# The branch rests in the last step of a half block, in the middle stage of a spectral/long-convolution kernel

## The chip, the cores and the metric

The kernel runs on one core of a Trainium2 chip. The core has a matrix engine (TensorE, PE in the profile; its weight loads are listed apart as PEld), a vector engine (VectorE, DVE), a scalar engine (ScalarE, ACT), a general engine (GpSimd, POOL) and an engine that here only issues transfers (SyncE, SP). Each engine works through its own instructions in order; semaphores tie the engines together. The metric is the time of the whole program on the device in microseconds, as the median of several runs.

## The reference

Four layers are applied to `x` of 2048 rows by 576 columns, twice the same pair. Layer A adds the real part of a two-dimensional Fourier transform of the normalised rows, done with given cosine and sine matrices. Layer B takes the normalised rows as a gate on a long causal convolution that doesn't depend on `x` at all:

```python
def _A_ref(x, dft_seq_re, dft_seq_im, dft_hid_re, dft_hid_im):
    a = jnp.einsum("bsd,ed->bse", x, dft_hid_re)
    b = jnp.einsum("bsd,ed->bse", x, dft_hid_im)
    return jnp.einsum("ts,bse->bte", dft_seq_re, a) - jnp.einsum("ts,bse->bte", dft_seq_im, b)

def _B_ref(q, k, v, shift_k, ssm_k, ssm_D):
    ...                     # k_shift: causal convolution of k, 4 taps
    kv = k_shift * v
    ...                     # y: causal convolution of kv with ssm_k, 2048 taps, by FFT
    y = y + kv * ssm_D[None, None, :]
    return q * y

x = x + _A_ref(_layernorm(x, axis=-1), ...)
x = x + _B_ref(_layernorm(x, axis=-1), ...)
x = x + _A_ref(_layernorm(x, axis=-1), ...)
x = x + _B_ref(_layernorm(x, axis=-1), ...)
```

## The kernel before

**Layer A in steps.** `layer` computes the sequence transform first. The 2048 output rows are four blocks of 512 (`tb`); each block has a half with the cosine matrix and a half with the sine matrix (`g`); each half block has 16 steps (`k`), numbered through as `n`, so that `n % 16` is the place in the half block and `n % 32 == 15` is the last step of a cosine half. A step multiplies one 128-row strip of `x` with one 128x512 piece of the matrix. Every operand is split in a rounded high part and a low part, so a step is 14 matmuls of 512 columns: three into each of the four accumulators (`s` in the profile) and two into a fifth (`rm`) for the 64 columns that are left over. There is one set of these accumulators. After the last step of a half, `evac_u` and `evac_r` move them to `u`, a high and a low part each: ScalarE copies (line 99), VectorE subtracts (line 100).

**The matrix pieces.** `load_c` asks for the piece of two steps ahead, through SP's queue (line 169 in the profile, `flts<-in_c_mat`, 256 KB), into one of two raw buffers; `split` then writes the high part on ScalarE (`mats<-flts`, line 99) and the low part on VectorE (`mats<-flts`, line 100) into one of three split buffers (`cs`). A raw buffer is free when VectorE's subtraction has read it; a split buffer is free when PE has finished the step that used it.

**The hidden transform.** When both halves of a block are there, `hidden` multiplies `u` with the second matrix: eight pieces of 27 matmuls a block (`bk<-w,u`), which `finish` lays between the steps of the next block.

**The branch.** `branch` is a generator that computes layer B's convolution beside layer A, since it needs no `x`. Its middle stage, which runs beside steps 47 to 111, has 64 "mid" feeds and 32 "i2" feeds. A mid feed is nine matmuls of 288 columns (`bk<-mid`, three each in `mid_kernel`, `mid_signal` and `mid_inverse`); ScalarE copies the results out of the accumulators (line 514, `flts<-bk`), moves half rows across (`flts<-flts`, 64x288, two of them) and splits (`mid<-flts`, 128x288 and 128x576); VectorE does lines 532 to 535 and the low parts of both splits (line 520). Feeds are read from DRAM through SP's queue (`flts<-td`, `mid<-td`), some feeds ahead, into a ring of land buffers; a land buffer is free when line 520 has read it. The copy `flts<-bk` of `mid_kernel` writes one of two `kk` buffers.

**What sets the order.** The generator of the layer yields inside each step: after the first and third accumulator ("part"), after the second (False) and at the end (True); in a last step after the second accumulator and at the end only. At each yield the program adds a share of the step to `passed`: 3/14, 3/14, 3/14 and 5/14 of `STEP` = 3.2, and 6/14 and 8/14 in a last step, times the weight in `BORDER` for that place. A finished hidden piece adds 3.6. Then the branch is advanced while its own count `spent` is under `work` times `passed / total`. The framework's scheduler makes each engine's final order from this, and may put neighbouring instructions in another order than the text has them; what it puts out is fixed when the program is built.

In the last step of a cosine half, `layer` also yields None while hidden pieces are left, and each such piece advances the branch too; that holds for any weight of `BORDER`.

Of the kernel before, what the change touches and what calls it, by code (L numbers as in the profile page):

```python
# [19 lines left out]
J = S // P  # L20
# [20 lines left out]
I2_END = 111  # L41
PREP = 113
MID_LAG = 1
BORDER = {J - 1: 0.5, 0: 0.75}
I2_FIRST = 37
I2_LATE = 6
I2_COST = 2.0
# [1 line left out]
STEP = 3.2  # L49
# [17 lines left out]
def fnet_h3_kernel(ctx: ExitStack, tc: tile.TileContext, x, c_mat, w_re, w_im, k_pad, v, shift_k,  # L67
# [34 lines left out]
    @contextmanager  # L102
    def behind(*instructions):
        with ExitStack() as stack:
            for i in instructions:
                stack.enter_context(tc.issue_after(i))
            yield
# [11 lines left out]
    def region_b(dt, name):  # L119
        return sb.tile([P, 6 * WIDE], dt, tag="rb", name=name)  # L120
# [11 lines left out]
    def lay(t, at, *sizes):  # L132

        for name, words, n in sizes:
            ring.setdefault(name, Ring()).tiles.extend(t[:, at + i * words:at + (i + 1) * words] for i in range(n))
            at += n * words
        assert at <= t.shape[1], (at, t.shape, sizes)
        return at

    def fresh(*names):  # L140
        for name in names:
            ring[name] = Ring()
# [150 lines left out]
    def finish(pending, pieces):  # L293
        while pending and pieces:
            if not isinstance(pending[0], types.GeneratorType):
                pending[0] = hidden(*pending[0])
            if next(pending[0], 0) == 0:
                pending.pop(0)
            else:
                pieces -= 1  # L300
# [432 lines left out]
    def advance(j=None):  # L733
        while to_store:
            load_after(*to_store.pop(0))
        with behind(*halved, *added, *evac):
            for row in list(making):
                if next(row, 0) == 0:
                    making.remove(row)
            if j is not None:  # L740
                making.append(make_x1(j))
                next(making[-1])
# [48 lines left out]
    for n, whole in layer(get_x0, lambda j: x[:, j, :], done0, pending):  # L791
        part = whole == "part"
        if part:
            whole = False
        if (whole or whole is not None and n % J < J - 1) and n <= F1_END and not part:
            at = n if whole else n - 0.5
            at16 = 4 + 2 * F1_16
            want = int(4 + F1_16 * at / 8 if at <= 16 else at16 + (68 - at16) * (at - 16) / (F1_END - 16))
            with behind(made[min(n + 2, J - 1)], *evac):
                while used < want:  # L800
                    next(br)
                    used += 1
        if whole is not None and not part and n >= W_FROM and len(W) < 9:
            with behind(*stored):
                next(wl)
        if whole and n == MID_LOAD:
            with behind(*asked):
                next(br)
        if n >= MID_FROM:
            if whole is not None:  # L810
                share = (5 if whole else 3) if n % J < J - 1 else (8 if whole else 6)
                passed += STEP * share / 14 * BORDER.get(n % J, 1.05)
            if whole is None or whole and n % 2 == 1 and n % (2 * J) < J - 1 and pending:
                finish(pending, 1)
                passed += PIECE
            while spent < work * min(1.0, passed / total):
                with behind(*added, *evac):
                    spent += next(br, work)
        if not whole:
            continue  # L820
        if n >= W_SAVE and n % 2 == 0:
            next(wl, 0)
        m = n - PREP
        if m == 0:
            lay(flts, SC_AT + CRAW * NT + 2 * D, ("xa", D, 2), ("yb", D, 2))
            old = ring["craw"]
            held = [old(), old()]
            fresh("craw")
            lay(flts, SC_AT + CRAW * NT + 6 * D, ("craw", NT, 1))
            ring["craw"].tiles.extend(held)  # L830
            gate = region_b(F32, "gate")
            lay(gate, 0, ("xa", D, 4), ("yb", D, 4), ("xj", D, 2))
        if 0 <= m and n < HOLD:
            advance(m // 2 if m % 2 == 0 and m < 2 * EARLY else None)
# [340 lines left out]
```

## Time and profile before

| | us |
|---|---|
| median of 3 runs | 1184.4 (1183.72 to 1184.5) |
| profiled execution, time | 1184.35 |
| profiled execution, span from first to last instruction | 1182.6 |
| middle stage in that span (steps 48 to 110) | about 250 to 604 |
| PE busy | 1168.9 (99% of the span) |
| VectorE busy | 866.5 (73%) |
| ScalarE busy | 647.7 (55%) |

Times in views of the trace are counted from the start of the span. A row of the chain or of a timeline gives its start, its length, the engine, the line and the tiles written and read, then the count; in brackets stands the idle time of the engine before it and what ended it. PE's matmuls overlap, so their listed lengths (about 0.39 us for 512 columns) are longer than the distance from one to the next; distances are read from the starts. `PEclk` is the share of full clock that PE was granted.

### The profile page before, as it was taken

The numbers are of one execution on the slowest core, as the hardware profiler recorded it, in microseconds if no ns is written. First come the engines' busy times: TensorE is split into PE (matmuls) and PEld (weight loads), VectorE is DVE, ScalarE is ACT, GpSimd is POOL, SyncE is SP. The second block draws the span as 40 slices with busy tenths as digits, with TensorE's granted clock in tenths as the row PEclk, the third lists the DMA queues.
The fourth block names the chain that finished last, engine by engine and source line by source line (L and its number), as shares of the span: only waits on it lengthen the run. The fifth ranks groups of instructions, "written<-read, shape, count | busy, mean of one in ns | idle before, by whom it ended". The sixth has DMA issues, their size and how long they took to land.

```text
span 1182.6 us, 18124 instructions
## 1 busy us (share of the span) xinstructions
PE 1168.9 (99%) x6198; PEld 990.9 (84%) x6198; DVE 866.5 (73%) x1564; ACT 647.7 (55%) x1280; POOL 75.5 (6%) x115
## 2 busy tenths in 40 slices
PE   8999999999999999999999999999999999999997
PEld 6776667987888988888888898888888888889997
DVE  7899984687777778877756765865776777774674
ACT  8855655577766667766645666534444445450210
POOL 2310000000000000001101111000000000001111
PEclk9999999999999999999999999999999999999999
DMA  9879898455766766648956777762772777895631
GB/s 331 290 235 310 270 300 283 146 158 156 216 201 192 211 181 189 187 142 237 287 188 213 250 242 236 250 242 79 253 247 72 236 269 257 264 322 158 198 108 40
DMA packets 147453, 255.64 MB, mean 216 GB/s; under 512 B 16161, under 2 KB 56353, under 8 KB 147362
## 3 DMA queue, kind: packets, MB, share of 16 engines
q1 hardware_dynamic: 111890, 210.17, 56.1%
q10 hardware_dynamic: 28560, 37.91, 9.1%
q0 software_dynamic: 6912, 6.43, 2.4%
q8 instruction: 48, 0.79, 0.3%
q14 instruction: 43, 0.35, 0.1%
HBM read 187.80 MB, written 66.65 MB: 215 GB/s over the span
## 4 chain that ended last, share of the span: by engine, by line
PE 92%; DMA 3%; DVE 2%; ACT 2%; issue 1%; SPq 0%; POOL 0%; DVEq 0%; ACTq 0%
PE s L76 54%; PE bk L76 30%; PE rm L76 6%; PE bf L76 3%; DMA flts<-in_c_mat 1%; DMA flts<-in_ssm_k 1%; DMA t<-ud 1%; ACT flts L514 1%; DMA early<-in_x 0%; DVE u L100 0%; DVE mats L100 0%; DVE mid L520 0%; ACT flts L453 0%; DMA flts<-td 0%; ACT mid L514 0%
## 5 line engine op out<-in xcount | busy, mean ns | idle before, releaser
L76 PE MATMUL s<-mats 128*128 128x512 f32 x2102 | 549.8, 395 | 3.1 <-ACT mats L197 1.6
L76 PEld LDWEIGHTS s<-mats 128*128 128x128 f32 x2102 | 383.1, 189 | 83.7 <-issue 10.8
L100 DVE TENSOR_TENSOR mats<-flts,mats 128x512 fp32r<-128x512 f32 x206 | 140.9, 688 | 58.7 <-ACT mats L99 57.3
L99 ACT ACTIVATE mats<-flts 128x512 fp32r<-128x512 f32 x206 | 128.4, 628 | 87.8 <-PE bk L76 30.2
L76 PE MATMUL bk<-mid 128*128 128x288 f32 x704 | 132.6, 303 | 2.6 <-ACT flts L514 2.2
L76 PEld LDWEIGHTS bk<-mid 128*128 128x128 f32 x704 | 111.5, 189 | 24.3 <-ACT flts L514 6.3
L514 ACT ACTIVATE flts<-bk 128x288 f32<-128x288 f32 (+1 forms) x192 | 78.3, 408 | 95.9 <-PE bk L76 80.4
L76 PE MATMUL bk<-w,u 128*128 128x288 f32 x864 | 119.9, 295 | 0.1
L76 PEld LDWEIGHTS bk<-w,u 128*128 128x128 f32 x864 | 117.5, 188 | 2.9 <-ACT flts L514 0.6
L520 DVE TENSOR_TENSOR mid<-flts,mid 128x576 fp32r<-128x576 f32 (+1 forms) x149 | 92.5, 624 | 9.1 <-ACT mid L514 6.7
L76 PE MATMUL rm<-mats 128*128 128x512 f32 x304 | 94.5, 391 | 0.0
L514 ACT ACTIVATE mid<-flts 128x576 fp32r<-128x576 f32 (+1 forms) x148 | 79.6, 574 | 3.5 <-DMA flts<-vd 1.6
L289 DVE TENSOR_TENSOR flts<-flts,bk 128x288 f32<-128x288 f32 x48 | 21.7, 453 | 69.1 <-PE bk L76 69.1
L76 PE MATMUL bk<-mats 128*128 128x288 f32 (+1 forms) x376 | 67.8, 317 | 0.0
L76 PEld LDWEIGHTS rm<-mats 128*128 128x128 f32 x304 | 57.0, 188 | 12.2 <-issue 0.2
L453 ACT ACTIVATE flts<-bf 128x384 f32<-128x384 f32 (+1 forms) x104 | 43.2, 461 | 43.9 <-PE bf L76 41.0
L76 PE MATMUL s<-t,mats 128*128 128x512 f32 x264 | 65.3, 390 | 0.3 <-DVE t L100 0.3
L186 POOL TENSOR_TENSOR flts<-flts 128x1 f32<-128x1 f32 x34 | 28.0, 823 | 517.6 <-DVE flts L185 515.2
L76 PE MATMUL bk<-mats,t 128*128 128x288 f32 (+1 forms) x368 | 59.3, 303 | 0.0
L76 PEld LDWEIGHTS s<-t,mats 128*128 128x128 f32 x264 | 49.4, 188 | 11.3 <-DVE t L100 0.8
L514 ACT ACTIVATE flts<-flts 64x288 f32<-64x288 f32 x128 | 56.6, 442 | 3.9
L76 PEld LDWEIGHTS bk<-mats 128*128 128x128 f32 x376 | 55.5, 188 | 3.4
(152 smaller groups left out, 1495.5 us busy)
## 6 DMA issues: line engine op xcount, KB each, us to landing
flts<-in_c_mat SPq DMA_DIRECT2D x148, 256.0 KB, 3.5
ph<-in_c_mat SPq DMA_DIRECT2D x54, 512.0 KB, 4.4
flts<-in_c_mat SPq DMA_DIRECT2D x30, 512.0 KB, 5.2
flts<-td SPq DMA_DIRECT2D x53, 288.0 KB, 3.1
td<-flts ACTq DMA_DIRECT2D x36, 384.0 KB, 4.3
vd<-flts ACTq DMA_DIRECT2D x64, 144.0 KB, 2.6
flts<-vd SPq DMA_DIRECT2D x32, 288.0 KB, 4.4
ud<-ph ACTq DMA_DIRECT2D x12, 512.0 KB, 6.4
```

What stands on the lines that cost most here:

```text
L76: return nc.tensor.matmul(ps, lhsT, rhs, start=first, stop=last, skip_group_check=more).ins
L99: a = nc.scalar.activation(h, src, AF.Copy).ins
L100: return a, nc.vector.tensor_tensor(l, src, h.bitcast(F32), OP.subtract).ins
L186: pows.append(nc.gpsimd.tensor_tensor(rs, ve, mhalf, OP.pow).ins)
L289: added[:] = [nc.vector.tensor_tensor(r[:, cs], r[:, cs], ps[:, :HD], OP.add).ins]
L453: stored[:] = [nc.scalar.activation(so[:, i, :], ps[i], AF.Copy).ins]
L514: last_act.append(nc.scalar.activation(*args, **kw).ins)
L520: nc.vector.tensor_tensor(l, src, h.bitcast(F32), OP.subtract)
```

## The change

Two weights of the shares change. The branch's weight in the last step of a half block goes from 0.5 to 0, the weight in the first stays at 0.75, and in the 14 others it goes from 1.05 to 1.085. A half block sums to 0.5 + 0.75 + 14 x 1.05 = 15.95 before and 0 + 0.75 + 14 x 1.085 = 15.94 now. Step 47, where the middle stage begins, is itself a last step.

```diff
-BORDER = {J - 1: 0.5, 0: 0.75}
+BORDER = {J - 1: 0.0, 0: 0.75}
...
                 share = (5 if whole else 3) if n % J < J - 1 else (8 if whole else 6)
-                passed += STEP * share / 14 * BORDER.get(n % J, 1.05)
+                passed += STEP * share / 14 * BORDER.get(n % J, 1.085)
```

No instruction is added or removed. What moves is the order.

The first place at which the orders part is just behind step 47. There, VectorE has the last subtraction of the fifth accumulator (`u<-flts`, 64x512), the four lines 532 to 535 of a branch feed, the two kinds of line 520, and the low parts of the matrix pieces (`mats<-flts`). Before:

```order
L100 TENSOR_TENSOR u<-flts,u 64x512
L532 SCALAR_TENSOR_TENSOR flts<-bk,flts 64x288
L520 TENSOR_TENSOR mid<-flts,mid 128x288
L533 TENSOR_TENSOR flts<-bk,flts 64x288
L534 TENSOR_TENSOR flts<-bk,flts 128x288
L520 TENSOR_TENSOR mid<-flts,mid 128x576
L535 TENSOR_TENSOR flts<-flts 128x288
L100 TENSOR_TENSOR mats<-flts,mats 128x512
L532 SCALAR_TENSOR_TENSOR flts<-bk,flts 64x288
L100 TENSOR_TENSOR mats<-flts,mats 128x512
```

VectorE at the same place now:

```order
L100 TENSOR_TENSOR u<-flts,u 64x512
L532 SCALAR_TENSOR_TENSOR flts<-bk,flts 64x288
L100 TENSOR_TENSOR mats<-flts,mats 128x512
L533 TENSOR_TENSOR flts<-bk,flts 64x288
L534 TENSOR_TENSOR flts<-bk,flts 128x288
L520 TENSOR_TENSOR mid<-flts,mid 128x288
L535 TENSOR_TENSOR flts<-flts 128x288
L520 TENSOR_TENSOR mid<-flts,mid 128x576
L532 SCALAR_TENSOR_TENSOR flts<-bk,flts 64x288
L100 TENSOR_TENSOR mats<-flts,mats 128x512
```

The first low part of a matrix piece stood behind one row of line 532 and five other branch rows; now it stands behind the row of line 532 alone.

SP's queue at the same place, as a piece of the difference (`td` are branch feeds, `in_c_mat` the matrix pieces):

```order
 L169 DMA flts<-in_c_mat 128x512
 L169 DMA mid<-td 128x576
-L169 DMA flts<-td 128x576
-L169 DMA flts<-in_c_mat 128x512 x2
+L169 DMA flts<-in_c_mat 128x512
+L169 DMA flts<-td 128x576
+L169 DMA flts<-in_c_mat 128x512
```

One matrix piece is asked for ahead of a branch feed instead of behind it.

ScalarE at the same place, from the second matrix piece split there (`mats<-flts`) to the third. Before:

```order
L99 ACTIVATE mats<-flts 128x512
L514 ACTIVATE flts<-flts 64x288
L550 DMA vd_80<-flts 128x288
L514 ACTIVATE flts<-flts 64x288
L514 ACTIVATE flts<-bk 128x288
L514 ACTIVATE mid<-flts 128x288
L514 ACTIVATE mid<-flts 128x576
L550 DMA vd_80<-flts 128x288
L514 ACTIVATE flts<-bk 128x288
L99 ACTIVATE mats<-flts 128x512
L514 ACTIVATE flts<-flts 64x288 x2
L514 ACTIVATE flts<-bk 128x288
```

And now:

```order
L99 ACTIVATE mats<-flts 128x512
L550 DMA vd_80<-flts 128x288
L514 ACTIVATE flts<-bk 128x288
L514 ACTIVATE flts<-flts 64x288 x2
L514 ACTIVATE flts<-bk 128x288
L514 ACTIVATE mid<-flts 128x288
L514 ACTIVATE mid<-flts 128x576
L99 ACTIVATE mats<-flts 128x512
L550 DMA vd_80<-flts 128x288
L514 ACTIVATE flts<-bk 128x288
L514 ACTIVATE flts<-flts 64x288 x2
L514 ACTIVATE flts<-bk 128x288
```

The third matrix piece has moved ahead of a copy `flts<-bk` and stands behind the split of a feed.

The third place is the border between steps 63 and 64. VectorE there has the four accumulators of the half that ends (`u<-s`). Before:

```order
L100 TENSOR_TENSOR u<-s_69,u 128x512
L535 TENSOR_TENSOR flts<-flts 128x288
L520 TENSOR_TENSOR mid<-flts,mid 128x288
L100 TENSOR_TENSOR u<-s_70,u 128x512
L520 TENSOR_TENSOR mid<-mid 128x576
L100 TENSOR_TENSOR u<-s_71,u 128x512
L100 TENSOR_TENSOR u<-s_72,u 128x512
```

Now:

```order
L100 TENSOR_TENSOR u<-s_69,u 128x512
L535 TENSOR_TENSOR flts<-flts 128x288
L100 TENSOR_TENSOR u<-s_70,u 128x512
L100 TENSOR_TENSOR u<-s_71,u 128x512
L100 TENSOR_TENSOR u<-s_72,u 128x512
```

Two rows of line 520 have moved from between the accumulators to behind them. On PE the three matmuls of a branch group that stood inside step 63 (behind its second accumulator) and the three between steps 63 and 64 now stand inside steps 64 and 65.

GpSimd's order is the same. PE's orders are the same up to step 49 and again from step 109 on.

## The prediction

> **What bounds the kernel now.** I read the page first: its span, PE's share, the chain that ended last.
>
> ```profile
> span 1182.6 us, 18124 instructions
> PE 1168.9 (99%) x6198; PEld 990.9 (84%) x6198; DVE 866.5 (73%) x1564; ACT 647.7 (55%) x1280; POOL 75.5 (6%) x115
> PE 92%; DMA 3%; DVE 2%; ACT 2%; issue 1%; SPq 0%; POOL 0%; DVEq 0%; ACTq 0%
> ```
>
> PE is busy 99% and is 92% of the chain, and the change takes no matmul away. So all that a new order can win is what PE stands still, or runs slowly, in the middle stage. The waits of PE come next: first of 259 to 276, behind step 47, then the whole list that PE's weight loads have from 276 to 604.
>
> ```profile
> PE bk L76 <- ACT flts L514: 2.2, 1, 2.2
> ```
>
> ```profile
> PEld bk L76 <- ACT flts L514: 2.8, 12, 0.5
> PEld bk L76 <- DVE flts L561: 1.4, 6, 0.4
> PEld s L76 <- DVE u L100: 0.3, 1, 0.3
> ```
>
> There is one wait of 2.2 us just behind the place where the orders part. After 276 no single one is over 0.5, the largest sum is 2.8, and the borders of half blocks show one wait for an accumulator, 0.3. Next the stretches of 3.41 us from the wait on, and an early one for comparison, with PE's busy time, then that of PEld, DVE, ACT and POOL, the granted clock, and the DMA's share and rate:
>
> ```profile
> 268.45:271.86 3.41, 1.27 (x7) 1.15 (x8) 2.57 (x6) 2.83 (x6) 0.00 (x0) 1.00 0.39 140
> 271.87:275.27 3.40, 3.40 (x13) 2.94 (x12) 3.29 (x8) 3.12 (x7) 0.00 (x0) 0.50 0.59 175
> 275.28:278.69 3.41, 3.41 (x20) 2.98 (x19) 1.95 (x5) 2.04 (x5) 0.00 (x0) 1.00 0.56 177
> 12.45:15.86 3.41, 2.23 (x11) 1.65 (x10) 3.41 (x14) 3.41 (x7) 2.63 (x5) 1.00 0.98 367
> ```
>
> The wait has a second price: in the stretch with PE busy for 1.27 us the clock is still full, in the next one it is 0.50 and 13 matmuls run where the one after it runs 20. The stretch at 12.45, with 2.23 busy, was not followed by a lower clock.
>
> Who caused the wait is read backwards. PE's timeline at both ends of the place, then ScalarE's timeline, then SP's queue, then VectorE's, then the chain's row of the transfer:
>
> ```profile
> 259.64 0.67 PE L76 MATMUL bk<-mid 128*128 128x288 f32 x3
> ...
> 270.59 0.66 PE L76 MATMUL bk<-mid 128*128 128x288 f32 x3 [2.24 <-ACT flts L514]
> ```
>
> ```profile
> 258.52 0.63 ACT L99 ACTIVATE u<-flts 64x512 fp32r<-64x512 f32 x1 [0.28 <-DVE flts L275]
> 259.18 0.41 ACT L514 ACTIVATE flts<-bk 128x288 f32<-128x288 f32 x1
> 259.48 1.01 ACT L514 ACTIVATE mid<-flts 128x288 fp32r<-128x288 f32 x2
> ...
> 266.08 0.41 ACT L514 ACTIVATE flts<-bk 128x288 f32<-128x288 f32 x1 [1.97 <-DVE mid L520]
> 268.53 0.63 ACT L99 ACTIVATE mats<-flts 128x512 fp32r<-128x512 f32 x1 [2.04 <-DMA flts<-in_c_mat]
> 269.19 0.91 ACT L514 ACTIVATE flts<-flts 64x288 f32<-64x288 f32 x2
> 270.12 0.41 ACT L514 ACTIVATE flts<-bk 128x288 f32<-128x288 f32 x1
> ```
>
> ```profile
> 257.24 0.32 SPq L169 DMA_DIRECT2D mid<-td  x1
> 262.50 0.32 SPq L169 DMA_DIRECT2D flts<-td  x1
> 263.47 2.56 SPq L169 DMA_DIRECT2D flts<-in_c_mat  x2
> ```
>
> ```profile
> 259.18 0.68 DVE L100 TENSOR_TENSOR u<-flts,u 64x512 fp32r<-64x512 f32 x1 [0.70 <-ACT u L99]
> 259.90 0.46 DVE L532 SCALAR_TENSOR_TENSOR flts<-bk,flts 64x288 f32<-64x288 f32 x1
> 260.88 0.45 DVE L533 TENSOR_TENSOR flts<-bk,flts 64x288 f32<-64x288 f32 x1
> 261.35 0.46 DVE L534 TENSOR_TENSOR flts<-bk,flts 128x288 f32<-128x288 f32 x1
> 261.72 0.75 DVE L520 TENSOR_TENSOR mid<-flts,mid 128x576 fp32r<-128x576 f32 x1
> 262.75 0.68 DVE L100 TENSOR_TENSOR mats<-flts,mats 128x512 fp32r<-128x512 f32 x1
> ```
>
> ```profile
> 263.47 4.98 DMA flts<-in_c_mat
> ```
>
> PE waits until 270.59 for the copy of 270.12. That copy stands on ScalarE behind the split of 268.53, which waited 2.04 us for a matrix piece (step 53's). The piece was asked for at 263.47 and took 4.98. It couldn't be asked for earlier: its raw buffer was read until 263.43 by VectorE's row of 262.75, which stood behind five branch rows though ScalarE's part of it was long done.
>
> **The change, part by part.**
>
> *The first low part moves up (step 51's piece, on VectorE).* In the new order it is the row behind line 532. Line 532 starts at 259.90 as before, since all before it is unchanged, and ends at 260.36; the row of 0.68 then ends at about 261.05 (ScalarE's half now stands right behind 259.15 and takes 0.63; the split buffer it writes is free when PE is done with step 48, before 259.64, so it ends by 260.3). The raw buffer is free at 261.05 instead of 263.43: 2.4 us earlier. On SP this request now stands right behind the one of 257.24, so it goes out at about 261.1. Lengths near by run from 2.9 to 5.0:
>
> ```profile
> DMA to landing us min/median/max: 2.9/4.4/5.0
> ```
>
> So it lands between 264.0 and 266.1, by the median at 265.5. On ScalarE the split that needs it now has ten rows between itself and 259.15: two splits of matrix pieces (0.63 each), three copies (0.41), the pair of half rows (0.91) and two pairs of feed splits (1.01 to 1.1): about 5.6 us, so it can't be reached before 264.8. ScalarE's wait there becomes 0 to 1.3 us, by the median 0.7, in place of 2.04.
>
> *Does PE notice?* The next two rows are a `kk` copy, which must wait for line 520 of an earlier product anyway (1.97 us at 266.08 before). Following VectorE's new order with the lengths above (four lines of 0.46, one 520 of 0.45 and one of 0.75, one low part of 0.68, about 3.7 a round), that line 520 ends near 266.1. Then ScalarE does the copy, the half rows and the next copy: 266.1 + 0.41 + 0.91 + 0.41 = 267.8. In PE's new order 28 matmuls of a step (0.23 us from start to start) and 18 of the branch (0.13) lie between 259.64 and the product that needs this accumulator, so PE gets there at 259.64 + 6.4 + 2.3 = 268.4 at the earliest. The margin is 0.6 us, and a piece that lands as late as 266.1 uses just that. So the gap goes: 2.24 us, by the bracket at 270.59.
>
> *The half clock behind it goes too.* At 0.50 for 3.41 us, PE lost 3.41 x 0.5 = 1.7 us. Without the gap the stretch before it is full. Even a gap of 1.2 would leave it as busy as the one at 12.45 that kept its clock.
>
> [...]
>
> *The branch feeds behind.* The `td` request now stands behind the matrix piece and its land buffer is read by line 520 ending near 263.6 instead of 262.47, so the request goes out 1.1 us later than 262.50. Feeds are asked for three ahead and a feed takes some 4 us, so 1.1 us is hidden; if it weren't, PE would lose up to 1.1. I take 0.
>
> *The rests at the borders.* Line 520 leaves the accumulators' rows; what PE can win is the row of 0.3 (`u L100`). It could lose the cover of the branch's matmuls: between the last product of an accumulator and its next use lie then nine matmuls of 0.23 and two of the fifth, 2.5 us; copy and subtraction need about 0.6 + 0.7 and a row of 0.45 between. That fits. I take 0, with -0.3 and +0.5 as ends.
>
> *Denser shares elsewhere.* 1.085 / 1.05 is 3.3% more branch a step. Windows of before, in the same columns:
>
> ```profile
> 291.50:322.10 30.60, 30.60 (x161) 26.24 (x160) 23.28 (x47) 22.59 (x50) 0.00 (x0) 1.00 0.67 197
> 444.10:499.90 55.80, 55.78 (x288) 47.82 (x287) 46.26 (x89) 40.15 (x87) 2.63 (x5) 1.00 0.68 192
> ```
>
> VectorE is busy 76% and 83%; 3.3% more makes 79% and 86%. The branch lags by three to seven matmuls behind each border and has caught up by the end of each half block, so PE's and the branch's total is the same. Weight loads wait 0.5 at most now; 3.3% on the 4.5 us listed first is 0.1. Bounds: -0.7 (a quarter of ScalarE's 2.8 falls away) to +1.5 (three new waits of 0.5). I take 0.1.
>
> Sum: -2.24 - 1.7 + 0.1 = -3.85. The profiled execution took 1184.35 us, 0.05 below the median of 1184.4, so both give about **1180.5 us**; its own range is 1179.3 to 1182.0.
>
> **The rivals.**
>
> *1. The wait moves instead of going.* The same burst, two matrix pieces split in a row, stands behind step 79. There the raw buffer comes free with this row, the next split is this one, and the pieces asked for between 436 and 448 took the time of the third line:
>
> ```profile
> 440.48 0.68 DVE L100 TENSOR_TENSOR mats<-flts,mats 128x512 fp32r<-128x512 f32 x1
> ...
> 444.47 0.63 ACT L99 ACTIVATE mats<-flts 128x512 fp32r<-128x512 f32 x1
> ...
> DMA to landing us min/median/max: 2.8/2.8/2.8
> ```
>
> From 441.2 to 444.47 are 3.3 us for a load of 2.8: a margin of 0.5. If other traffic now falls there and the load takes 5.0, ScalarE waits 1.7, PE perhaps as long, and with the half clock 1.7 more. 1180.5 + 1.7 to 3.4 = 1182.2 to 1183.9. Against it: the two matrix pieces and the rows between them are in the same order there.
>
> [...]
>
> *3. VectorE becomes the bound in the dense steps: slower.* Its 76 to 83% are means; its order is fixed, and it also waits within a feed for ScalarE. A dense step has 3.2 x 1.085 / 3.1 = 1.12 mid feeds, so 14 x 0.23 + 1.12 x 9 x 0.13 = 4.5 us of PE, or 4.0 a feed; VectorE needs 3.0 us for a feed and 0.6 for its share of a matrix piece. The slack is 0.4 us a feed. If VectorE's waits in the new order exceed 0.4, PE is held by the rest: 0.15 us on each of some 64 mid feeds is 10 us, so 1180.5 + 10 = 1190; from 0.1 a feed on it is slower than before. Against it: at 83% in 444 to 500 PE lost 0.02 of 55.8 us.
>
> *4. The change does nothing that shows:* PE's wait stays, for the same copy, because the load takes 7 us and the margin above is gone: 1184.4. Against it: the longest load here took 5.0.
>
> **How the numbers follow.** 0.2% is 2.4 us, about what a measurement of this kernel can tell from no change. Forecast 0.64, rival 1 0.10, rival 2 0.06, rival 3 0.15, rival 4 0.05. The forecast's range lies within "faster" up to 1182.0; rivals 1, 2 and 4 are "same". So faster 0.64, same 0.21, slower 0.15. The range leaves out rival 3 and a little at the low end: 1179.0 to 1185.0; the likeliest case alone has 1179.3 to 1182.0.
>
> **What would show it.** In the profile after: a matrix piece asked for near 261.1 and no wait of ScalarE over 1.3 us at its split; no PE wait of 2.2 between 259 and 276; the clock 1.0 throughout the middle stage; step 109's products some 3.9 us earlier than before. The forecast is wrong if a wait of 1.5 us or more with a clock of 0.50 behind it stands anywhere between 259 and 604, or if the weight loads' waits for ScalarE and VectorE sum to several times 2.8 and 1.4.

## The result, and the profile after

| | before | after |
|---|---|---|
| median, us (11 runs each) | 1184.4 (1182.17 to 1186.27) | 1180.36 (1180.09 to 1181.87) |
| profiled execution, time | 1184.35 | 1181.27 |
| its span | 1182.6 | 1179.5 |

The ratio is 0.9971 (95%: 0.9962 to 0.998): faster by 4.0 us. The page of the profile after begins so (span, engines, chain by engine):

```profile
span 1179.5 us, 18144 instructions
PE 1167.0 (99%) x6198; PEld 988.8 (84%) x6198; DVE 867.0 (74%) x1564; ACT 647.6 (55%) x1280; POOL 75.7 (6%) x115
PE 90%; DVE 4%; DMA 3%; ACT 2%; issue 1%; SPq 0%; POOL 0%; DVEq 0%; ACTq 0%
```

The work is the same (6198 matmuls) and PE is still the bound. The 20 instructions that the page counts more are all semaphore instructions: of those that compute or move data none is added or removed. PE's waits from 259 to 276, where the 2.2 us stood, and then the rows of its weight loads from 276 to 604 that the prediction shows for the kernel before:

```profile
PE rm L76 <- DVE flts L275: 0.3, 1, 0.3
```

```profile
PEld bk L76 <- ACT flts L514: 4.4, 18, 0.5
...
PEld bk L76 <- DVE flts L561: 0.7, 4, 0.2
PEld s L76 <- DVE u L100: 0.4, 1, 0.4
...
```

PE's wait for the copy of line 514 is gone. The 0.3 us that is there now comes ahead of the place where the orders part; the kernel before shows it too when it is profiled again (0.5, first experiment), so it is no effect of the change. The windows of the same place, columns as in the prediction (length, PE, PEld, DVE, ACT, POOL, clock, DMA share, GB/s):

```profile
262.01:265.42 3.41, 3.41 (x19) 2.84 (x19) 3.31 (x7) 2.52 (x6) 0.00 (x0) 1.00 0.42 120
265.43:268.83 3.40, 3.40 (x20) 2.70 (x19) 3.34 (x7) 2.97 (x7) 0.00 (x0) 1.00 0.77 199
268.84:272.25 3.41, 3.41 (x20) 2.94 (x20) 3.23 (x8) 3.26 (x8) 0.00 (x0) 1.00 0.68 219
```

Every stretch has 19 or 20 matmuls at full clock, where before had one of 7 and then one of 13 at 0.50.

How the piece comes in time is read along the prediction's steps: SP's queue, the length of the load of step 53's piece and then of all loads from 256 to 276, VectorE, ScalarE, PE.

```profile
262.58 0.33 SPq L169 DMA_DIRECT2D flts<-in_c_mat  x1
264.93 0.32 SPq L169 DMA_DIRECT2D flts<-td  x1
```

```profile
DMA to landing us min/median/max: 2.6/2.6/2.6
```

```profile
DMA to landing us min/median/max: 2.6/2.8/3.5
```

```profile
260.65 0.68 DVE L100 TENSOR_TENSOR u<-flts,u 64x512 fp32r<-64x512 f32 x1 [0.70 <-ACT u L99]
261.36 0.46 DVE L532 SCALAR_TENSOR_TENSOR flts<-bk,flts 64x288 f32<-64x288 f32 x1
261.86 0.69 DVE L100 TENSOR_TENSOR mats<-flts,mats 128x512 fp32r<-128x512 f32 x1
...
267.01 0.45 DVE L520 TENSOR_TENSOR mid<-flts,mid 128x288 fp32r<-128x288 f32 x1
```

```profile
266.50 0.62 ACT L99 ACTIVATE mats<-flts 128x512 fp32r<-128x512 f32 x1
267.49 0.41 ACT L514 ACTIVATE flts<-bk 128x288 f32<-128x288 f32 x1 [0.37 <-DVE mid L520]
267.94 0.92 ACT L514 ACTIVATE flts<-flts 64x288 f32<-64x288 f32 x2
268.88 0.41 ACT L514 ACTIVATE flts<-bk 128x288 f32<-128x288 f32 x1
```

```profile
270.51 0.55 PE L76 MATMUL bk<-mid 128*128 128x288 f32 x3
```

This execution runs about 1.5 us later at this place (the `u` row starts at 260.65, before at 259.18): 1.0 of it is there from the first steps of the program, and 0.5 comes just ahead of this place, where a copy of ScalarE waited for a `vd` store (0.5 here, 0.7 when the kernel before was profiled again). So the rows are compared by their distance from that row, and the two spans differ by only 3.1. The low part ends at 262.55 and the request follows at 262.58. The piece landed at 265.2, and ScalarE's split at 266.50 carries no bracket: it didn't wait. The copy that frees the accumulator ends at 269.29, and PE takes it at 270.51, with no bracket.

**Where the time went.** From the first fifth-accumulator product of step 48 to that of step 111 every kernel here runs the same 1910 matmuls. In undisturbed stretches of the traces a matmul starts 0.229 us (512 columns) or 0.132 us (288) after the one ahead of it. What each distance has beyond that, added up from the starts in the traces, is the loss, split here at 3 and 20 us after the start of step 48:

| profiled execution | all, us | loss 0 to 3 | loss 3 to 20 (the place of the gap) | loss from 20 to step 111 |
|---|---|---|---|---|
| before | 348.1 | 0.2 | 4.6 | 6.7 |
| after | 343.6 | 0.4 | 0.6 | 6.1 |

Of 4.4 us, 4.0 come from the place behind step 47 and 0.6 from all the rest of the middle stage. At step 111 this execution is 3.0 us ahead, at the end 3.1.

### The profile page after: what moved, and what is told of

It is laid out like the page before. It is cut to its first block, busy times and chain, and to the rows that moved or that the text cites. A ratio compares the mean times of both kernels' runs of the same rounds, so it can differ in the third digit from the quotient of the medians.

```text
span 1179.5 us, 18144 instructions
## 1 busy us (share of the span) xinstructions
PE 1167.0 (99%) x6198; PEld 988.8 (84%) x6198; DVE 867.0 (74%) x1564; ACT 647.6 (55%) x1280; POOL 75.7 (6%) x115
## 4 chain that ended last, share of the span: by engine, by line
PE 90%; DVE 4%; DMA 3%; ACT 2%; issue 1%; SPq 0%; POOL 0%; DVEq 0%; ACTq 0%
PE s L76 52%; PE bk L76 29%; PE rm L76 6%; PE bf L76 2%; DMA flts<-in_ssm_k 1%; DMA t<-ud 1%; DVE f1f L395 1%; ACT flts L514 1%; DVE mid L520 0%; DVE mats L100 0%; DVE f1f L400 0%; DMA early<-in_x 0%; DVE u L100 0%; DMA vd<-flts 0%; DMA flts<-vd 0%
```

## The experiments

All times are medians in us, and each ratio is to the kernel before on the same chip. `e1` to `e4` ran on one chip (the kernel before took 1183.86 there), `e5` to `e8` on a second (1183.93), `e9` to `e11` on a third (1184.76).

| | time | ratio (95%) | middle stage, us | loss 3 to 20 | loss from 20 |
|---|---|---|---|---|---|
| e1, before again | 1184.19 | 1.0001 (0.9991 to 1.0011) | 347.3 | 3.1 | 7.4 |
| e2, rest at 47 only | 1181.52 | 0.9979 (0.9968 to 0.9989) | 343.9 | 0.6 | 6.4 |
| e3, all but the rest at 47 | 1184.84 | 1.0007 (0.9998 to 1.0016) | 347.2 | 3.4 | 7.1 |
| e4, denser shares only | 1186.02 | 1.0017 (1.0007 to 1.0028) | 350.4 | 4.8 | 8.8 |
| e5, rests only | 1181.93 | 0.9977 (0.9968 to 0.9985) | 343.6 | 0.6 | 6.1 |
| e9, before without one load | 1182.0 | 0.998 (0.9971 to 0.9989) | 344.1 | 0.8 | 6.6 |
| e10, after again | 1180.73 | 0.9971 (0.996 to 0.9981) | 343.7 | 0.6 | 6.2 |
| e11, rest at 47 only, again | 1180.71 | 0.9969 (0.9958 to 0.998) | 343.7 | 0.6 | 6.2 |

The last three columns are those of the table above, each from the one profiled execution. `e6` to `e8` stand in their own section.

### The kernel before once more

> The kernel before, unchanged, for its spread. My theory (one gap of 2.2 us behind step 47 and a stretch at half clock that follows it in a fixed window): every execution has the gap; where the window cuts it in two, the half clock is missing and the span is 1.7 us shorter with a mean clock higher by 0.0014. So two groups of spans, near 1182.6 and 1180.9, median of the times 1184.4. If the half clock always follows the gap: one group only, and the 4 us between the shortest and longest of the 11 runs come from elsewhere, with no relation to the clock.

The gap is there again; PE's row, and then the windows from it on:

```profile
271.18 0.66 PE L76 MATMUL bk<-mid 128*128 128x288 f32 x3 [2.27 <-ACT flts L514]
```

```profile
267.08:270.49 3.41, 1.83 (x9) 1.25 (x8) 1.17 (x2) 1.31 (x3) 0.00 (x0) 1.00 0.45 142
270.49:273.91 3.42, 2.73 (x15) 2.39 (x16) 3.34 (x7) 2.83 (x7) 0.00 (x0) 1.00 0.42 120
273.91:277.32 3.41, 3.41 (x20) 2.94 (x19) 3.26 (x8) 3.15 (x9) 0.00 (x0) 1.00 0.66 207
```

The half clock is not. In these traces the records of the granted clock start whole numbers of 3.413 us apart (here at 7.65 and 1178.42; in the kernel before at 5.62, 271.87, 275.28 and 1179.81; in the changed one at 5.48 and 1176.25), and the stretches shown are cut on that grid. Here a line of the grid falls in the middle of the gap, so the gap is shared by one stretch with 1.83 us of PE work and one with 2.73, and neither was followed by 0.50. The loss at the place is 3.1 instead of 4.6: between two executions of the same program, one with the half clock and one without, lie 1.5 us.

How often it comes can be read from the mean clock that each run records, to three places. One stretch at half clock takes 3.41 x 0.5 / 1182.6 = 0.0014 off it, and the 0.50 at the very end of every profile here (2.2 to 4.6 us) another 0.0010 to 0.0020. So I estimate that a run at 0.999 has no such stretch, that one at 0.997 or less has one, and that 0.998 can be either; the profiles with the stretch are at 0.997 (before, `e5`) and 0.998 (`e4`), `e1` and `e3` without it at 0.998, the changed kernel at 0.999. Of the 82 runs of the kernel before in these experiments, 28 are at 0.997 or less, with a median span of 1183.4, 32 at 0.999, with 1181.6, and 22 between. The two groups that were expected are there, 1.8 us apart. Of 73 runs of the kernels without the gap one is at 0.997, and its profile shows the stretch near the start of the program (`e5` below). So by this estimate between a third and three fifths of the runs of the kernel before pay for the half clock.

### The rest behind step 47 alone

```diff
-                passed += STEP * share / 14 * BORDER.get(n % J, 1.05)
+                passed += STEP * share / 14 * (0.0 if n == MID_FROM else BORDER.get(n % J, 1.05))
```

`MID_FROM` is 47. One step rests; every other weight is that of before.

> Only the weight of step 47 goes to 0; every other share is as before. Theory (the whole gain is the gap and half clock behind step 47): 1180.4 to 1180.8, no PE wait over 1.2 us between 259 and 276, clock 1.0 throughout. Rival (the gain is shared by the rests at all four borders, about 1 us each): 1183.4. Rival (the denser shares make the gain): 1184.4.

> Only step 47 rests, once more, beside the changed kernel. Theory (step 47 is all of it): no difference to the changed kernel that exceeds 0.8 us, so 1180.4 to 1181.2. Rival (the other rests with the denser shares are worth about 1 us of their own): 1181.4 to 1182.0.

Windows at the place, of the first of the two, and the lengths of the loads there:

```profile
265.41:268.82 3.41, 3.41 (x20) 2.81 (x19) 3.35 (x7) 2.95 (x8) 0.00 (x0) 1.00 0.71 204
268.82:272.23 3.41, 3.41 (x19) 2.86 (x18) 3.24 (x8) 3.10 (x7) 0.00 (x0) 1.00 0.65 209
```

```profile
DMA to landing us min/median/max: 2.6/3.1/3.3
```

No gap, full clock, and the loss at the place is that of the changed kernel. The first time it measured 0.9979; beside the changed kernel on one chip the two gave 1180.71 and 1180.73. As far as these runs can tell kernels apart, the rest behind step 47 is the whole gain.

### Everything but that rest

```diff
-BORDER = {J - 1: 0.5, 0: 0.75}
+BORDER = {J - 1: 0.0, 0: 0.75}
...
-                passed += STEP * share / 14 * BORDER.get(n % J, 1.05)
+                passed += STEP * share / 14 * (0.5 if n == MID_FROM else BORDER.get(n % J, 1.085))
```

> The whole change except at step 47, which keeps its weight of 0.5. Theory: the order behind step 47 is that of before, the gap of about 2.2 us and the half clock stay: 1184.4, within 0.6. Rival (rests at all borders): 1181.4. Rival (denser shares): 1180.5.

ScalarE's split of the late piece, PE's wait and the windows:

```profile
269.37 0.63 ACT L99 ACTIVATE mats<-flts 128x512 fp32r<-128x512 f32 x1 [2.09 <-DMA flts<-in_c_mat]
```

```profile
PE bk L76 <- ACT flts L514: 2.3, 1, 2.3
```

```profile
266.63:270.04 3.41, 2.53 (x12) 1.81 (x12) 1.19 (x4) 1.06 (x3) 0.00 (x0) 1.00 0.63 187
270.04:273.45 3.41, 2.03 (x11) 1.83 (x12) 3.31 (x7) 2.81 (x7) 0.00 (x0) 1.00 0.42 125
```

With the three other rests and the denser shares in, and that one rest out, the gap is back and the time is that of before. Here again the gap lay over two stretches and the clock stayed full.

### The denser shares alone

```diff
-                passed += STEP * share / 14 * BORDER.get(n % J, 1.05)
+                passed += STEP * share / 14 * BORDER.get(n % J, 1.085)
```

> Only the 14 weights of 1.05 go to 1.085; the last steps keep 0.5. Theory: gap and half clock behind step 47 stay, the denser shares cost nothing: 1184.4 to 1184.9. Rival (denser shares make the gain): 1180.5. Rival (denser shares cost, and the rests more than pay for it): 1186 or more.

Windows at the gap, and waits of the weight loads from 276 to 604:

```profile
269.32:272.73 3.41, 1.04 (x6) 0.86 (x6) 2.20 (x5) 2.83 (x6) 0.00 (x0) 1.00 0.39 117
272.74:276.14 3.40, 3.40 (x11) 2.84 (x11) 3.10 (x7) 2.56 (x7) 0.00 (x0) 0.50 0.53 161
```

```profile
PEld bk L76 <- ACT flts L514: 5.8, 15, 1.1
...
PEld s L76 <- DVE u L100: 0.6, 2, 0.4
```

Slower by 2.2 us at the medians. The gap and, this time, the half clock are there (4.8 lost at the place), and the rest of the stage loses 8.8 instead of 6.7. Without the rests a half block's weights sum to 0.5 + 0.75 + 14 x 1.085 = 16.44 instead of 15.95: the branch is driven ahead of its pace by 3%, and PE's weight loads wait for ScalarE up to 1.1 us at once. PE's order shows the lead: from step 48 to step 95 it has 472 matmuls of the mid feeds here, 457 in the kernel before and 454 in the changed one. That the lead causes the waits is argued from this and was not tested alone. In the change itself the weights sum to 15.94.

### The rests alone

```diff
-BORDER = {J - 1: 0.5, 0: 0.75}
+BORDER = {J - 1: 0.0, 0: 0.75}
```

> Only the weight of the last steps goes to 0, the 14 others stay 1.05 (so the branch ends a little later). Theory: the order behind step 47 is the new one, gap and half clock are gone: 1180.4 to 1181. Rival (the denser shares are needed, since without them the branch's end sticks out behind step 111): 1182 or more, with PE running branch matmuls behind step 111.

The gap is gone and the middle stage is as short as with the whole change. The denser shares aren't needed for it. One stretch near the start of this execution is of use below:

```profile
7.83:11.24 3.41, 1.93 (x10) 1.02 (x10) 3.14 (x9) 1.23 (x3) 0.00 (x0) 1.00 1.03 349
11.25:14.65 3.40, 3.40 (x12) 2.53 (x9) 3.05 (x14) 3.02 (x6) 2.52 (x4) 0.50 1.01 357
```

### The piece late again, in the new order

To make the gap of a chosen size, an extra store of `u` to scratch memory in DRAM (`extra_d`) was put on SP's queue in the changed kernel, ahead of the request for step 53's piece. The line shown stores 512 KB; with 7 and 5 in place of 8 it is 1 MB and 2 MB.

```diff
-        raw = ring["craw"]()
+        raw = ring["craw"](); [load_after(extra_d, um[0][:, 8 * WIDE:9 * WIDE].bitcast(F32)) for _ in range(step == (1, 1, 5))]
```

> The changed kernel with one extra store of 512 KB (the last part of u to a scratch in DRAM) in SP's queue right ahead of the request for step 53's matrix piece; PE, VectorE and ScalarE have the same order as the changed kernel. Theory: the piece lands some 1.6 us later, near 267, ScalarE waits 0.5 to 0.9 us, PE's margin of 0.6 takes nearly all of it: PE gap 0 to 0.4, no half clock, 1180.4 to 1180.9. Rival (a late piece always costs PE its own lateness): 1182.

> The same with a store of 1 MB. PE's order is that of the changed kernel; on ScalarE the split of step 53's piece stands one copy later. Theory: the piece lands near 268.6, PE gap about 1 us, the 3.41 us around it stay over 60% busy, no half clock: 1181 to 1182. Rival (any gap of about 1 us brings the half clock): 1183.2 or more.

> The same with a store of 2 MB; PE's order is unchanged, on ScalarE and VectorE the pieces of steps 53 and 54 are split later. Theory: the piece lands near 272, PE gap 2 to 4 us and the half clock with it, 1.7 us more: 1184 to 1186. [...]

They took 1180.49 (0.9966; 0.9953 to 0.9979), 1180.03 (0.996; 0.9948 to 0.9973) and 1180.58 (0.9964; 0.995 to 0.9977): no loss in any. The load that follows the store of 512 KB (262 to 265), the one behind 1 MB (261 to 263), and the two behind 2 MB (262 to 267):

```profile
DMA to landing us min/median/max: 2.8/2.8/2.8
```

```profile
DMA to landing us min/median/max: 4.4/4.4/4.4
```

```profile
DMA to landing us min/median/max: 5.9/6.5/7.2
```

512 KB hardly delayed the load (2.8 against 2.6 without a store). 2 MB made the loads longer than the 4.98 of before, but in the order that was built with the added store ScalarE's split stands elsewhere (ScalarE's timeline with 2 MB):

```profile
267.72 0.41 ACT L514 ACTIVATE flts<-bk 128x288 f32<-128x288 f32 x1 [0.94 <-DVE mid L520]
...
269.11 0.41 ACT L514 ACTIVATE flts<-bk 128x288 f32<-128x288 f32 x1
...
270.59 0.41 ACT L514 ACTIVATE flts<-bk 128x288 f32<-128x288 f32 x1 [0.16 <-DVE mid L520]
...
271.50 0.63 ACT L99 ACTIVATE mats<-flts 128x512 fp32r<-128x512 f32 x1
```

The split stands behind three copies, and PE had no wait for ScalarE. So these runs didn't set the size of a gap, which they were meant to; they show something else. With 2 MB step 53's piece, requested at 262.75, took 7.2 us and landed 9.7 us after the first fifth-accumulator product of step 48 (260.28); in the kernel before it landed 9.8 after it (268.45 against 258.64), in the changed one 5.1. A piece as late as that of before cost PE nothing here, because the copies that PE needs next stand ahead of its split.

### Before, without the load that comes late

```diff
-        anchor.append(load_after(raw, c_mat[g, tb, k]) if anchor else nc.sync.dma_start(raw, c_mat[g, tb, k]).ins)
+        if step != (1, 1, 5): anchor.append(load_after(raw, c_mat[g, tb, k]) if anchor else nc.sync.dma_start(raw, c_mat[g, tb, k]).ins)
```

> The kernel before without one transfer: step 53's matrix piece isn't loaded, the split works on what the raw buffer held (so step 53's products are those of another piece). VectorE frees the raw buffer as late as before; of all rows only two neighbours on ScalarE and two on VectorE change places, and a few on PE and SP. Theory (the load that came 2 us late was the whole gap): no PE wait over 0.6 us behind step 47, clock 1.0, 1180.5 to 1182. Rival (the rows of VectorE that the old order put ahead, not the load, hold ScalarE and PE): a gap of 1.5 us or more stays, 1183 to 1184.5.

ScalarE's split of the piece, and PE's waits from 259 to 276:

```profile
266.41 0.64 ACT L99 ACTIVATE mats<-flts 128x512 fp32r<-128x512 f32 x1 [0.53 <-PE rm L76]
```

```profile
PE rm L76 <- DVE flts L275: 0.3, 1, 0.3
```

The shares are those of before and the order has no rest, but with no load to wait for, the split waits only 0.5 us, for PE to free its buffer, the copy behind it is in time, and the gap and the half clock are gone. That the split and the first of its two neighbouring copies have changed places isn't what does it: counted from the first fifth-accumulator product of step 48 (258.64 before, 260.40 here) that copy starts at 7.4 in both, and the second, the one that PE needs, at 11.5 before and 8.8 here. The loss at the place falls to 0.8. The gain, 2.8 us, is less than the 4.0 of the change beside it; the loss from 20 us on is 0.4 above that of the changed kernel, and the loss at the place 0.2, which are parts of it.

### The changed kernel once more

> The changed kernel once more, beside the next one. Theory: 1180.4, 3 to 4 us under the kernel before.

It took 1180.73: a gain of 4.03, as in the result (4.04). No wait of 2 us and no lower clock stand between 259 and 604; the middle stage took 343.7.

No run gives the kernel before a third raw buffer, which would let the request go out early without any new order.

## Why the prediction was right

Predicted 1180.5, measured 1180.36. The mechanism is the one given; that the number was met to 0.1 us is in part luck, since a term that only some of the runs pay was counted in full and some small losses behind the place, for which the sum has +0.1, fell away too. Step by step:

- **The low part moves up and the request goes out earlier.** Predicted 1.92 us after the `u` row (261.1 against 259.18), measured 1.93 (262.58 against 260.65). Right.
- **The piece lands in time.** The step holds, its size was off: I took 4.4 us of 2.9 to 5.0 and so a ScalarE wait of 0.7 in 0 to 1.3; the piece took 2.6 (the other loads there up to 3.5) and landed 4.5 us after the `u` row, ahead of the 4.8 to 6.9 that I gave, and ScalarE didn't wait. The 4.98 was a load of the old order, asked for 1 us behind a feed; now the feed is asked for 2.4 us behind the piece. I carried a duration from a place where its neighbours were others; that these set the length was not tested.
- **Does PE notice?** The three points of the chain, as distances: end of line 520, 6.9 predicted and 6.81 measured (267.46); end of the copy, 8.6 and 8.64 (269.29); PE at the product, 9.2 at the earliest and 9.86. The margin is 1.2 us instead of 0.6. That the late piece is the cause, by way of ScalarE's order, is shown from three sides: taking away the load takes away the gap, of the change's parts only the one that moves that load does, and with 2 MB stored ahead a piece that is as late leaves no gap where ScalarE's order is another.
- **The gap, 2.24 us.** Its place shows 2.4 to 2.5 us more from one start to the next than an undisturbed pair in all four executions with the gap. Right.
- **The half clock, 1.7 us.** Of the right size where it comes (4.6 - 3.1 = 1.5 between two executions of the same program), but not part of every execution: it followed the gap in two of four profiles (before and `e4`, not `e1` and `e3`). The sum counted it in full, from one execution that had it and took the median's time; a median of three says little of a term that comes and goes. By the estimate from the mean clocks above, between a third and three fifths of the runs of the kernel before pay it, so on the average it is worth 0.6 to 1.1 us and not 1.7. On the chip of the last comparison the 7 runs of the kernel before at 0.999 have a median of 1183.58, and the 7 at 0.997 one of 1185.24; against 1180.73 the gain is 2.9 without the half clock and 4.5 with it. The medians of all runs happen to give the full sum in the comparisons on the chips of the result and of the last three runs (4.03 to 4.05), and 2.0 to 2.3 in `e2` and `e5`. What came on top of the gap without the half clock is seen in `e1` and `e3`: their middle stage is 3.6 us longer than that of the changed kernel, 2.5 to 2.8 of it at the place and 0.9 to 1.3 in small losses after it, of which 0.7 is what two executions of the kernel before differ by (6.7 and 7.4). Where those small losses come from stays open.
- **Feeds, and rests at the other borders: 0.** The `td` request went out at 264.93, and no wait for a feed shows. The three other rests and the denser shares together made no measurable difference (`e3`: 1.0007; `e10` against `e11`: 0.02 us). Right.
- **Denser shares, +0.1, bounds -0.7 and +1.5.** In the change the loss from 20 us on went from 6.7 to 6.1, within the bounds. The list of waits that the prediction calls whole is three rows of seven: all seven sum to 7.0 us and not 4.5, so 3.3% of it is 0.2. In the change the sum is 8.0: the waits for ScalarE's line 514 copies rose from 2.8 to 4.4 in 18 small ones instead of 12, those for line 561 fell from 1.4 to 0.7. So here the waits of the weight loads (up 1.0) don't tell what PE loses (down 0.6). Alone, the denser shares cost 2.2 us (`e4`), above my upper bound. I had costed them as if they stood alone, from VectorE's busy share, but alone they drive the branch ahead of its pace, and the rests take just that away again.
- **Rivals 1, 3 and 4** didn't come: the matrix pieces from step 79 on make PE wait nowhere, VectorE's denser steps don't hold it, and the wait went. Rival 3 was costed too dear: a dense step has 9 matmuls of the mid feeds in either order (steps 50 to 56), that is one feed and not 1.12, since the program also scales the share by `work / total` = 262.4 / 294.4. With one feed a step I estimate 4.4 us for PE (14 x 0.229 + 9 x 0.132) and 3.6 for VectorE (the prediction's 3.0 + 0.6), a slack of 0.8 instead of 0.4.

## What to carry to other kernels

When one wait of a busy engine stands alone, read it backwards over every queue until something is late for no good reason: here a ring's buffer was held 2.4 us by the last of its readers, which stood behind work of another stream, and 256 KB came late through two engines' orders. A weight in a planner may work by the single row it moves: test the parts one at a time, because the other parts of this change did nothing, or harm when alone. The same gap of 2.2 to 2.4 us in the matrix engine had a half clock behind it in two of four profiles, and two executions of one program differed by 1.5 us for it, so one profile with a half clock behind a gap doesn't tell what the median pays; the mean clocks of all timed runs gave bounds for it.

## What the runs showed of the hardware

- **The clock after a gap.** Stretches of 3.41 us with PE busy for 1.27 (before) and 1.04 us (`e4`) were followed by one at 0.50, those with 1.83 and 2.73 (`e1`) and 2.53 and 2.03 us (`e3`) in the middle stage were not. At the start of `e5` 1.93 us were, and at 12.45 of the kernel before 2.23 were not. So no single bound on the busy time that the profile shows fits all of these; what decides it stays open. No profile here has two stretches at 0.50 in a row behind the gap.
- **Loads behind a store.** A 256 KB load asked for behind a store on the same queue took 2.8 us when the store was 512 KB, 4.4 when it was 1 MB and 7.2 when it was 2 MB; without a store it took 2.6 in the changed order. Without a store the 256 KB loads from 256 to 276 took 2.6 to 5.1 us over the kernels before and after and `e1` to `e5`, in orders that differ in what is asked for beside them; which neighbour sets the length wasn't taken apart.
